# An mLSTM cell and an MLP in one kernel: where y of the twelve later units is transposed

## The chip, the cores and the metric

The kernel runs on one core of a Trainium2 chip. The metric is the device time of one execution in microseconds (us). Engines are named as in the profile: PE is TensorE (PEld its weight loads), DVE is VectorE, ACT is ScalarE, POOL is GpSimd, SP is SyncE, which here only issues DMAs.

## What is computed

An mLSTM cell over 4 batches, 8 heads, 768 steps and a head dimension of 40, followed by an MLP over 3072 tokens (320 features, 2048 hidden):

```python
def _attn_ref(q, k, v, i_gate, f_gate, o_gate):
    ...
    for t in range(S):
        ...
        m_new = np.maximum(f_gate[:, :, t] + m, i_gate[:, :, t])
        f_stab = np.exp(f_gate[:, :, t] + m - m_new)
        i_stab = np.exp(i_gate[:, :, t] - m_new)
        m = m_new
        C = f_stab[:, :, None, None] * C + i_stab[:, :, None, None] * np.einsum('bhd,bhe->bhde', vt, kt)
        n = f_stab[:, :, None] * n + i_stab[:, :, None] * kt
        h_tilde = np.einsum('bhde,bhe->bhd', C, qt)
        nq = np.einsum('bhd,bhd->bh', n, qt)[:, :, None]
        denom = np.maximum(np.abs(nq), 1.0)
        o = 1.0 / (1.0 + np.exp(-o_gate[:, :, t]))
        y[:, :, t] = o * h_tilde / denom
    return y
...
    x = np.ascontiguousarray(attn_out.transpose(0, 2, 1, 3)).reshape(B * S, H * D)
    h = x @ w_in
    g = h - np.tanh(h)
    return (g @ w_out).astype(np.float32)
```

Everything is float32.

## The kernel before

**Units and groups.** The tokens are cut into 24 units of 128 (a chunk of one batch; unit n is chunk n // 4 of batch n % 4). The cell of one unit makes `y`, 128 tokens by 320 features, tokens in the partitions. The MLP works on groups of two units (12 groups of 256 tokens) and needs x with features in the partitions. Six tiles `xT` (L324), each 128 partitions by 3 blocks by 256 tokens, hold it, one to a group in turn (group g uses `xT[g % 6]`). The three blocks start at the features in `FROM` (L276): 0, 128 and 192. The last two overlap; the second is read at its lower 64 rows and the third at its upper 64, as a half-height product each.

**The cell of a unit.** `scores` (L620) makes q times k by heads in PSUM (`ps` in the profile), a mask brings it to SBUF as `P`; `inter` and `intra` (L654, L663) add the state's part and the chunk's own part in `ph`; `gate` (L668) divides and multiplies by the output gate on VectorE and leaves `y` in one of two tiles `ys`; `update` (L694) computes the new state in `pc`, which `keep_state` (L702) adds and scales on VectorE. Then x: `turn` (L711) transposes one 128-column block of `y` on TensorE into PSUM tile `px`, and the third call ends with `keep_x` (L719), a ScalarE copy of 128 by 384 into the unit's half of `xT`.

**PSUM in the later part.** `ph`, `pc` and `px` come from `small` (L312), which takes turns over the banks named in `banks`. From L1374 on, one of the two serves the MLP's sums and the list has one name, so these three tiles follow each other in one bank.

**The MLP of an item.** An item is two pairs of 128-column blocks of the hidden layer, for one group. `up` (L897) makes `ph_up` from `xT` and `w_in`: 8 full-height products and 4 half-height ones, 24 passes in the profile. `shrink` squares on ScalarE (`z`, `q`), then VectorE makes `gt` in two steps, first out of `ph_up` and `z`, then out of `q`; `sums_of_g` (L770) makes the sums `s`, and `down_seven` (L785) multiplies into `pS` in 14 products, 28 passes, one item later.

**Order of the work.** Units 0 to 11 are laid out by a planner with costs (class Plan, L157); the change does not touch it. From item START on, the loop at L1376 merges two lists by hand: the dense products of an item, and the steps of a slot. A slot (s, o) with o = s - 1 covers two items; it finishes unit o and loads and prepares the next ones. `cell_slot` (L723) lists a slot's steps with a cost in us: inter and intra, gate, five pauses, three updates and four pauses (units 12 to 19), three turns, pauses, `prepare(s)`. `spread_over` (L1361) sets them at equal distances over the two items, and `merge` (L1011) places each at its share of the item's dense cost. `Clock` (L135) adds up the costs and releases the steps that `shrink` put off. Each engine runs its instructions in the order in which they are issued by these lists (L96 to L133), each engine by itself: an engine waits only where it needs another's result or a free buffer.

**SP's queue.** `load_unit` (L342) issues a unit's ten loads (seven where k is not needed) on SP at the beginning of a slot, for unit s + 1: kz and qz in two halves each, v, k, o, and q by heads in three parts (`q2`). The tiles have three buffers (o four), and SP issues a load as soon as its buffer is free. SP does nothing else in this stretch; the outputs go out on ACT's queue.

**A second path.** L1502 to the end recomputes all in a general way if a bound on the arguments fails; it is not run with these inputs, and it keeps using `turn`.

Of the kernel before, what the change touches and what calls it, by code (L numbers as in the profile page):

```python
# [49 lines left out]
FP = mybir.dt.float32  # L50
# [10 lines left out]
L = 128  # L61
# [18 lines left out]
def kernel(  # L80
# [33 lines left out]
    V, A, SP, G = Pinned(nc.vector), Pinned(nc.scalar), Pinned(nc.sync), Pinned(nc.gpsimd)  # L114
# [161 lines left out]
    FROM = (0, 128, DM - 128)  # L276
    NK = 2
    HALF = 64
    assert FROM[1] + HALF == FROM[2]
    NU = B * NT  # L280
    GT = 2
# [15 lines left out]
    NX = FIRST + 2  # L297
# [3 lines left out]
    dram = ctx.enter_context(tc.tile_pool(name="dram", bufs=1, space=bass.MemoryType.DRAM))  # L301
    att = ctx.enter_context(tc.tile_pool(name="att", bufs=2))
# [9 lines left out]
    def small(shape, name):  # L312
        banks.append(banks.pop(0))
        return ps_b.tile(shape, FP, name=name, tag=banks[-1])
# [9 lines left out]
    xT = [const.tile([128, NK + 1, TG], FP, name=f"xT{i}") for i in range(NX)]  # L324
# [17 lines left out]
    def load_unit(n, names=("kz", "qz", "v", "k", "o", "q2"), queue=SP, behind=()):  # L342
        c, b = divmod(n, B)
        t = ld.setdefault(n, {})
        for name in names:
            if name in ("kz", "qz"):
                t[name] = load.tile([128, HH, L], FP, name=name, tag=name, bufs=3)
                for i in range(2):
                    src = kT if name == "kz" else qT
                    dma = queue.dma_start(out=t[name][i * HALF:i * HALF + D], in_=src[b, c, :, i * HH:(i + 1) * HH])  # L350
                    if behind:
                        tc.add_manual_dep(dma.ins, behind[-1].ins.name, SYNC, reason="order of transfers")
            elif name == "k":
                if n + B < NU:
                    t["k"] = load.tile([L, WIDE, D], FP, name="k", tag="k", bufs=3)
                    queue.dma_start(out=t["k"].rearrange("p h d -> p (h d)"),
                                    in_=bass.AP(k.tensor, k[b, c].offset, [[H * D, L], [1, WIDE * D]]))
            elif name != "q2":
                src, bufs = {"v": (v, 3), "o": (o_gate, 4)}[name]
                t[name] = load.tile([L, H, D], FP, name=name, tag=name, bufs=bufs)  # L360
                queue.dma_start(out=t[name], in_=src[b, c])
            elif c:
                t["q2"] = load.tile([TOP, len(TRIOS), L], FP, name="q2", tag="q2", bufs=3)
                for i in range(TRIO):
                    queue.dma_start(out=t["q2"][i * D:(i + 1) * D, 0:len(range(i, H, TRIO))], in_=qT[b, c, :, slice(i, H, TRIO)])
# [204 lines left out]
    part = [parts_of[n // GT][:, n % GT] for n in range(FIRST * GT)]  # L570
# [3 lines left out]
    un = {}  # L574
# [12 lines left out]
    def begin(n):  # L587
        if n in ld:
            arrive(n)

        un[n]["P"] = att.tile([L, 2, HH, L], FP, name="P", tag="P", bufs=4)
# [5 lines left out]
    def prepare(n, whole=True, by_heads=False):  # L597

        t = un[n]
        if "vs" in t:  # L600
            return
        t["vs"] = scaled(n, 0, "vs", 4, by_heads)
        if whole:
            t["column"]()
            open_gate(n)
# [48 lines left out]
    def inter(n, j):  # L654
        t = un[n]
        if "ph" not in t:
            t["ph"] = small([L, H, D1], "ph")
        if t["c"]:
            rows = slice(0, len(TRIOS[j]) * D)
            T.matmul(trio(t["ph"], j), t["qs"][rows, j, :], trio(state[t["b"]][t["c"] % 2][rows], j), start=(j == 0), stop=False,  # L660
                     skip_group_check=True)

    def intra(n, h):  # L663
        t = un[n]
        T.matmul(t["ph"][:, h, :], t["P"][:, h // HH, h % HH, :], t["vs"][:, h, :], start=(t["c"] == 0 and h == 0), stop=True,
                 skip_group_check=True)

    def gate(n, in_parts=False):  # L668

        t = un[n]  # L670
        ph, sg = t["ph"], t["o"]
        den = att.tile([L, H], FP, name="den", tag="den")


        def over():
            V.scalar_tensor_tensor(out=den, in0=ph[:, :, D], scalar=-1.0, in1=inv[:, t["c"], t["hs"]], op0=OP.mult, op1=OP.max)
            V.tensor_tensor(out=den, in0=den, in1=ph[:, :, D], op=OP.max)
            V.reciprocal(out=den, in_=den)

        def shares():  # L680
            for h in range(H):
                A.mul(out=sg[:, h], in_=sg[:, h], mul=den[:, h:h + 1])

        def product():
            y = t["y"] = ys[n % 2]
            V.tensor_tensor(out=y.rearrange("p (h d) -> p h d", d=D), in0=ph[:, :, 0:D], in1=sg, op=OP.mult)

        if in_parts:
            return over, shares, product
        over()  # L690
        V.tensor_tensor(out=sg, in0=sg, in1=den.unsqueeze(2).to_broadcast([L, H, D]), op=OP.mult)
        product()

    def update(n, j, at_once=True):  # L694
        t = un[n]
        if j == 0:
            t["pc"] = small([TOP, H, D1], "pc")
        T.matmul(trio(t["pc"], j), t["k"][:, TRIO * j:TRIO * (j + 1)].rearrange("p h d -> p (h d)"), trio(t.get("vs_end", t["vs"]), j), start=True, stop=True)
        if j == len(TRIOS) - 1 and at_once:
            keep_state(n)  # L700
# [10 lines left out]
    def turn(n, j, at_once=True):  # L711
        t = un[n]
        if j == 0:
            t["px"] = small([128, NK + 1, L], "px")
        T.transpose(t["px"][:, j, :], t["y"][:, FROM[j]:FROM[j] + 128], ident)
        if j == NK and at_once:
            keep_x(n)

    def keep_x(n):  # L719
        g, tt = divmod(n, GT)  # L720
        A.copy(out=xT[g % NX][:, :, tt * L:(tt + 1) * L], in_=un[n]["px"])

    def cell_slot(s, o):  # L723


        steps, pause = [], [(0.0, lambda: None)]
        if o is not None:
            prepare(o)
        if s is not None:
            if s + 1 < NU and s + 1 not in ld:  # L730
                load_unit(s + 1)
            begin(s)
        if o is None:
            return [(0.0, lambda: prepare(s))]
        for d, heads in enumerate(TRIOS):
            steps.append((0.22 if o >= B else 0.0, lambda d=d: inter(o, d)))
            steps += [(0.22, lambda h=h: intra(o, h)) for h in heads]
        steps.append((0.0, lambda: gate(o)))
        steps += 5 * pause
        if o + B < NU:  # L740
            steps += [(0.2, lambda j=j: update(o, j)) for j in range(len(TRIOS))] + 4 * pause
        steps += [(0.11, lambda j=j: turn(o, j)) for j in range(NK + 1)] + 2 * pause
        if s is not None:
            steps.append((0.0, lambda: prepare(s)))
        return steps + 2 * pause
# [151 lines left out]
    def up(some, shrink):  # L897

        n = len(some)
        ph = [ps_h.tile([128, 2, TG], FP, name="ph_up", tag=f"ph{i}") for i in range(2)]  # L900

        def product(i, x, j):
            g, p = some[x]
            f = 2 * p + i
            at = ((0, 2, 1), (0, 1, 2))[i][j]
            if j < NK:
                col = (i, 3 - i)[j]
                lhs, rhs = w_in[:, p, col * 128:(col + 1) * 128], xT[g % NX][:, at, :]
            else:
                rows = slice(i * HALF, (i + 1) * HALF)  # L910
                lhs, rhs = w_in[rows, p, 2 * NK * 128:], xT[g % NX][rows, at, :]
            T.matmul(ph[i][:, x, :], lhs, rhs, start=(x == 0 and j == 0), stop=(j == NK), skip_group_check=True)

        full = [(0.43, lambda i=i, x=x, j=j: product(i, x, j)) for i in range(2) for x in range(n) for j in range(NK)]
        rest = [lambda i=i, x=x: product(i, x, NK) for x in range(n) for i in range(2)]
        return full, (rest, [lambda: shrink(some, ph)])
# [185 lines left out]
    of_tokens, of_states, exponentials, rows = {}, {}, [], []  # L1102
# [131 lines left out]
    for p in range(SPLIT, NP):  # L1234
        steps = []
# [266 lines left out]
    with tc.If(loaded[0] > 0):  # L1502
# [17 lines left out]
        for g in range(NG):  # L1520
# [19 lines left out]
            for p0 in range(0, NP, 2):  # L1540
                gts = []
                full, half = up(((g, p0), (g, p0 + 1)), lambda _, phs: gts.extend(shrink_any(ph) for ph in phs))
# [8 lines left out]
            for tt in range(GT):  # L1551
                o = mlp.tile([128, 5, HM], FP, name="ob", tag="ob")[:, 0:2].rearrange("p two n -> p (two n)")
# [43 lines left out]
```

## Time and profile before

| | us |
|---|---|
| median of 3 runs | 537.22 |
| lowest, highest | 537.08, 545.9 |
| profiled execution | 536.48 |
| its span, first to last instruction | 534.7 |
| units 12 to 23 (slots), in the span | some 231 to 474 |
| one slot (two items) with an update | 21.26 |
| mean granted TensorE clock | 0.996 |

The page gives busy times of each engine, the span in 40 slices, the DMA queues, the chain of work that ended last, and the costliest groups of instructions. A group's row has the engine, operation, output and input tiles, shape, count, then busy time in us, mean ns of one, and the idle time of the engine ahead of it with what ended it. In the timeline the first number is the start, the second the length, both in us; in brackets stands the idle time before it. A float32 product appears as two passes, a transpose as one: three transposes of 24 units are 72 matmuls. L106 and L129 are helpers that record every instruction, so the tiles' names tell the groups apart.

These groups of 231 to 474 us say what the engines do beside the cell's chain:

```profile
L106 DVE SCALAR_TENSOR_TENSOR gt<-q,gt 128x512 f32<-128x512 f32 x48 | 31.4, 683 | 0.0
L106 DVE SCALAR_TENSOR_TENSOR gt<-ph_up,z 128x512 f32<-128x512 f32 x48 | 30.8, 683 | 31.2 <-ACT z L106 31.2
L106 DVE TENSOR_TENSOR P<-ps,upto 128x512 f32<-128x512 f32 x21 | 13.6, 686 | 57.0 <-PE ps L129 57.0
L106 ACT COPY xT<-px 128x384 f32<-128x384 f32 x12 | 5.7, 472 | 0.0
```

VectorE spends most of its time on gt, and waits for ScalarE's z and TensorE's ps.

### The profile page before, as it was taken

How to read it: one execution, taken by the hardware profiler on the slowest of the kernel's cores; microseconds unless marked ns; L12 is line 12 of the kernel's file. 1: busy time of each engine (PE TensorE's matmuls, PEld its weight loads, DVE VectorE, ACT ScalarE, POOL GpSimd, SP SyncE). 2: the span in 40 equal slices, each digit the busy share in tenths (PEclk: the TensorE clock that was granted, in tenths of full speed). 3: DMA queues.
4: the chain of work that ended last, by engine and by line, in shares of the span. 5: the costliest groups of instructions: out<-in, count | busy, mean ns of one | idle time of the engine just before them, and what ended most of it. 6: DMA issues, size and time to landing. Idle time of an engine off the chain costs nothing.

```text
span 534.7 us, 9279 instructions
## 1 busy us (share of the span) xinstructions
PE 527.0 (99%) x3541; PEld 461.4 (86%) x3541; DVE 355.0 (66%) x768; ACT 204.3 (38%) x521; POOL 36.0 (7%) x63
## 2 busy tenths in 40 slices
PE   8999999999999999999999999999999999999996
PEld 5778878888798889889998998999999989988885
DVE  4999889988757666855853854756646546555544
ACT  4475696655442424223213312332242233232312
POOL 4523233100000000000000000000000000000000
PEclk8999999999999999999999999999999999999999
DMA  7987656331210001011302202111110000000001
GB/s 230 277 247 221 186 158 192 116 112 38 75 40 26 25 16 48 25 43 35 101 2 74 89 14 89 61 46 42 38 50 13 2 26 0 1 26 0 26 1 29
DMA packets 28137, 37.97 MB, mean 71 GB/s; under 512 B 3576, under 2 KB 21816, under 8 KB 28088
## 3 DMA queue, kind: packets, MB, share of 16 engines
q1 hardware_dynamic: 21856, 22.57, 14.6%
q0 software_dynamic: 3040, 10.82, 6.5%
q10 hardware_dynamic: 3192, 3.93, 2.2%
q8 instruction: 30, 0.49, 0.4%
q14 instruction: 19, 0.16, 0.1%
HBM read 33.37 MB, written 3.93 MB: 70 GB/s over the span
## 4 chain that ended last, share of the span: by engine, by line
PE 96%; DVE 1%; ACT 1%; POOL 1%; DMA 0%; issue 0%; SPq 0%; DVEq 0%
PE ph_up L129 41%; PE pS L129 30%; PE ph L129 9%; PE po L129 7%; PE ps L129 4%; PE pc L129 2%; PE px L133 2%; PE awake L129 1%; DMA w_out<-in_i_gate 0%; POOL w L106 0%; ACT vs L106 0%; DVE w_in L106 0%; ACT L106 0%; PE gate L129 0%; POOL P L106 0%; DVE den L106 0%
## 5 line engine op out<-in xcount | busy, mean ns | idle before, releaser
L129 PE MATMUL ph_up<-xT,w_in 128*128 128x256 f32 (+1 forms) x1152 | 245.2, 391 | 0.0
L129 PEld LDWEIGHTS ph_up<-xT,w_in 128*128 128x128 f32 (+1 forms) x1152 | 169.0, 189 | 28.7 <-issue 12.2
L106 ACT ACTIVATE z<-ph_up 128x512 f32<-128x512 f32 (+1 forms) x98 | 56.7, 583 | 255.9 <-PE ph_up L129 138.6
L106 DVE SCALAR_TENSOR_TENSOR gt<-ph_up,z 128x512 f32<-128x512 f32 (+1 forms) x98 | 63.4, 675 | 79.4 <-ACT z L106 79.1
L129 PE MATMUL pS<-wT,s 128*128 128x160 f32 x480 | 73.1, 300 | 0.0
L129 PEld LDWEIGHTS pS<-wT,s 128*128 128x128 f32 x480 | 67.5, 190 | 0.0
L106 DVE TENSOR_TENSOR P<-ps,upto 128x512 f32<-128x512 f32 x36 | 23.3, 686 | 66.5 <-PE ps L129 66.5
L106 ACT ACTIVATE q<-z,tiny 128x512 f32<-128x512 f32 (+1 forms) x98 | 66.2, 711 | 1.0
L106 DVE SCALAR_TENSOR_TENSOR gt<-q,gt 128x512 f32<-128x512 f32 (+1 forms) x98 | 63.4, 681 | 0.0
L129 PEld LDWEIGHTS ph<-vs,P 128*128 128x128 f32 x384 | 56.9, 191 | 5.7 <-POOL P L106 0.9
L129 PE MATMUL pS<-w_out,gt 128*128 128x160 f32 x320 | 56.8, 310 | 0.0
L129 PE MATMUL ph<-vs,P 128*128 128x41 f32 x384 | 55.4, 261 | 0.4 <-POOL P L106 0.4
L129 PEld LDWEIGHTS pS<-w_out,gt 128*128 128x128 f32 x320 | 46.1, 192 | 4.8 <-issue 3.6
L129 PE MATMUL po<-w_out,gt 128*128 128x320 f32 x128 | 38.2, 441 | 0.0
L129 PEld LDWEIGHTS po<-w_out,gt 128*128 128x128 f32 x128 | 23.1, 190 | 8.5 <-issue 0.3
L106 DVE TENSOR_TENSOR s<-gt 128x256 f32<-128x256 f32 x80 | 30.2, 418 | 0.0
L129 PE MATMUL pS<-wT,gt 128*128 128x160 f32 x160 | 29.2, 301 | 0.0
L129 PE MATMUL pS<-w_out,s 128*128 128x160 f32 x160 | 28.3, 299 | 0.0
L129 PEld LDWEIGHTS ps<-qz,kz 40*128 40x128 f32 x384 | 25.8, 191 | 2.2 <-DVE vs L106 0.8
L129 PE MATMUL ps<-qz,kz 40*128 40x128 f32 x384 | 26.6, 277 | 0.0
L129 PEld LDWEIGHTS pS<-w_out,s 128*128 128x128 f32 x160 | 23.9, 190 | 0.0
L129 PEld LDWEIGHTS pS<-wT,gt 128*128 128x128 f32 x160 | 23.8, 190 | 0.0
(93 smaller groups left out, 476.2 us busy)
## 6 DMA issues: line engine op xcount, KB each, us to landing
w<-in_moe_w_out POOLq DMA_DIRECT2D x8, 640.0 KB, 6.2
w<-in_moe_w_in POOLq DMA_DIRECT2D x16, 256.0 KB, 4.5
kz<-in_kT SPq DMA_DIRECT2D x48, 80.0 KB
o<-in_o_gate SPq DMA_DIRECT2D x24, 160.0 KB
k<-in_k SPq DMA_DIRECT2D x20, 180.0 KB
qz<-in_qT SPq DMA_DIRECT2D x44, 80.0 KB
v<-in_v SPq DMA_DIRECT2D x22, 160.0 KB
out<-ob ACTq DMA_DIRECT2D x11, 320.0 KB
```

The source lines that it names most:

```text
L106: i = method(*args, **kwargs)
L129: return cls.keep(nc.tensor.matmul(*args, **kwargs))
L133: return cls.keep(nc.tensor.transpose(*args, **kwargs))
```

## The change

In `cell_slot` the three `turn` steps of cost 0.11 become one step of cost 0, `turn_by_store`. It turns y's blocks of 32 by 32 on VectorE into a tile `yt`: each block is transposed where it stands, so partition 32 a + i, block b, column j holds feature 32 b + i of token 32 a + j. Four DMAs on SP, one for each 32 partitions, write the blocks into a DRAM tile `y_rows` of 384 features by 128 tokens, in runs of 32 tokens (128 B); two more DMAs on SP read the rows into the two halves of the partitions of `xT`. `yt` has two buffers, `y_rows` four. The planner's units and the second path keep `turn` and `keep_x`.

```diff
+    BLOCK = 32
+    NB = (NK + 1) * 128 // BLOCK
+
+    def turn_by_store(n):
...
+        y, g, tt = un[n]["y"], *divmod(n, GT)
+        yt = att.tile([L, NB, BLOCK], FP, name="yt", tag="yt")
+        flat = yt.rearrange("p b j -> p (b j)")
+        V.transpose(flat[:, 0:NK * 128], y[:, 0:NK * 128])
+        V.transpose(flat[:, NK * 128:], y[:, FROM[NK]:])
+        rows = dram.tile([(NK + 1) * 128, L], FP, name="y_rows", tag=f"y_rows{n % 4}")
+        for a in range(L // BLOCK):
+            part = slice(a * BLOCK, (a + 1) * BLOCK)
+            SP.dma_start(out=rows[:, part].rearrange("(b i) j -> i b j", i=BLOCK), in_=yt[part])
+        for i in range(2):
+            half = slice(i * HALF, (i + 1) * HALF)
+            SP.dma_start(out=xT[g % NX][half, :, tt * L:(tt + 1) * L], in_=rows.rearrange("(c p) t -> p c t", p=128)[half])
+
     def cell_slot(s, o):
...
-        steps += [(0.11, lambda j=j: turn(o, j)) for j in range(NK + 1)] + 2 * pause
+        steps += [(0.0, lambda: turn_by_store(o))] + 2 * pause
         if s is not None:
             steps.append((0.0, lambda: prepare(s)))
         return steps + 2 * pause
```

## Prediction

> **What bounds the kernel now.** I read the page from the top: busy times, the clock row, the chain of waits.
>
> ```profile
> ## 1 busy us (share of the span) xinstructions
> PE 527.0 (99%) x3541; PEld 461.4 (86%) x3541; DVE 355.0 (66%) x768; ACT 204.3 (38%) x521; POOL 36.0 (7%) x63
> ...
> PEclk8999999999999999999999999999999999999999
> ...
> PE 96%; DVE 1%; ACT 1%; POOL 1%; DMA 0%; issue 0%; SPq 0%; DVEq 0%
> PE ph_up L129 41%; PE pS L129 30%; PE ph L129 9%; PE po L129 7%; PE ps L129 4%; PE pc L129 2%; PE px L133 2%; PE awake L129 1%; DMA w_out<-in_i_gate 0%; POOL w L106 0%; ACT vs L106 0%; DVE w_in L106 0%; ACT L106 0%; PE gate L129 0%; POOL P L106 0%; DVE den L106 0%
> ```
>
> The chain that ended last is 96% TensorE at full clock. So a TensorE instruction taken away shortens the run by the time between starts that it took, and work on another engine costs nothing until TensorE waits for it. The list of waits for PE between 231 and 474 us, where the twelve later units run, is empty: there is no wait to remove, only work. The groups, with shapes kept apart, give the work that the change touches, for all 24 units:
>
> ```profile
> L133 PE MATMUL px<-ident,ys 128*128 128x128 f32 x72 | 16.4, 285 | 0.2 <-DVE ys L106 0.2
> L106 ACT COPY xT<-px 128x384 f32<-128x384 f32 x24 | 11.2, 476 | 13.5 <-PE px L133 13.5
> ```
>
> Half of each belongs to units 12 to 23. The 285 ns is a latency in a pipeline, not what the end would gain. What one set of three costs is read by comparing items (24 ph_up and 28 pS passes each) in TensorE's timeline; the first number is the start:
>
> ```profile
> 465.77 3.62 PE L129 MATMUL ph_up<-xT,w_in 128*128 128x256 f32 x16
> 469.22 0.27 PE L133 MATMUL px<-ident,ys 128*128 128x128 f32 x1
> ...
> 470.49 0.33 PE L133 MATMUL px<-ident,ys 128*128 128x128 f32 x1
> 470.66 0.71 PE L129 MATMUL pS<-w_out,gt 128*128 128x160 f32 x4
> 471.20 0.27 PE L133 MATMUL px<-ident,ys 128*128 128x128 f32 x1
> 471.31 0.71 PE L129 MATMUL pS<-w_out,gt 128*128 128x160 f32 x4
> ...
> 474.57 4.68 PE L129 MATMUL ph_up<-xT,w_in 128*128 128x256 f32 x24
> ...
> 483.09 4.68 PE L129 MATMUL ph_up<-xT,w_in 128*128 128x256 f32 x24
> ```
>
> The item with unit 23's three transposes lasts 474.57 - 465.77 = 8.80 us, the next, without any, 483.09 - 474.57 = 8.52. Three transposes cost **0.28 us**, not 3 x 0.285.
>
> **What the Trainium skill says.** "TensorE: Matmul & The Clock Gate", Part 4, puts a TensorE transpose inside a kernel at about 275 ns; the trace's median is 273. "VectorE: DVE Perf Modes", The three transpose paths, gives VectorE 311 ns for 128x128 in bf16 and says that it turns 32x32 blocks only, which is why the blocks must be put in their places by a transfer; no such instruction is in this trace. "DMA: Bandwidth & Descriptors", Specifications, says that under 512 B the engines read, modify and write; Anatomy of one DMA puts a fixed 2.0 us on each transfer, mostly the receipt of the write. The stores here have runs of 128 B; the trace has no such store to agree or not.
>
> **The change, part by part**, for each of 12 units.
>
> Removed from TensorE: three transposes, 0.28 us; 12 x 0.28 = 3.4 us. Bounds: the chain charges px 1.8% of 534.7 us over 24 units, 0.40 each, 4.8 in all, and part of that is a switch from the 64-row products that stays; 36 whole durations of 273 ns would be 9.8 us, which the overlap excludes. Below, nothing is gained if the gap stays. I take 3.4.
>
> Removed from ScalarE: a copy of 476 ns. ScalarE is 38% busy and not on the chain: 0.
>
> Removed from PSUM: px no longer takes the one rotating bank between pc and the next unit's ph. No wait there shows today: 0.
>
> Added on VectorE: turns of 128x256 and 128x128. Nearest rows: a product of 128x256 out of SBUF is 418 ns, a copy of 128x128 284; together **0.70 us**. The skill's 311 ns per block of 128 columns would give 0.93; at half that rate for four-byte data 1.87 (estimates). I take 0.7 and keep 0.6 to 1.9. They stand in VectorE's order after the state update and ahead of the next gt out of ph_up:
>
> ```profile
> 260.17 0.50 DVE L106 TENSOR_TENSOR state<-state,eT 120x328 f32<-120x328 f32 x1
> 261.99 1.29 DVE L106 SCALAR_TENSOR_TENSOR gt<-ph_up,z 128x512 f32<-128x512 f32 x2 [1.32 <-ACT z L106]
> ...
> 265.52 0.82 PE L129 MATMUL ph_up<-xT,w_in 128*128 128x256 f32 x3
> ```
>
> VectorE idles 1.32 us there, waiting for ScalarE's z, and 0.7 fits inside. Should it not, gt is late; the next product into that bank starts at 265.52, 2.24 us after gt ends at 263.28. So TensorE feels only what goes past 1.32 + 2.24 = 3.6 us. For units without an update the idle is 3.40 us (before gt at 410.29), for unit 23 1.73. Cost: 0. Its waits for y are on its own engine; behind it stand gt, s and vs, with their users an item away.
>
> Added on SP's queue: four stores and two loads. A head-sliced load takes 0.38 us to issue (three in 1.15), so 2.3 us in all. The first store waits for the turns; the first x load waits for all stores to land. Queued behind are the loads of unit o+3, which today go out as soon as buffers allow:
>
> ```profile
> 258.38 0.35 SPq L106 DMA_DIRECT2D k<-in_k  x1
> ...
> 260.76 0.71 SPq L106 DMA_DIRECT2D kz<-in_kT  x2
> ```
>
> k at 258.38 is unit 16's, released by unit 13's update; the kz behind it is already unit 17's. In the new order unit 16's kz waits for unit 13's round trip, unit 17's for unit 14's, a slot later than today. The round trip from the page's queue rows:
>
> ```profile
> q1 hardware_dynamic: 21856, 22.57, 14.6%
> q10 hardware_dynamic: 3192, 3.93, 2.2%
> ```
>
> 14.6% of 16 engines' 534.7 us over 21856 packets is 57 ns a packet; q10, which writes the output, has 59. Four stores are 4 x 384 = 1536 packets, 96 an engine: 5.5 us at 57 ns, 11 at double. The two x loads are 384 packets, 1.4 us. With 2 us fixed for the stores and again for the loads, x is in SBUF 1.6 + 2 + 5.5 + 0.8 + 2 + 1.4 = 13.3 us after the turns (18.8 at double).
>
> Who waits: group 6 begins with unit 13's x at 286.78 in TensorE's timeline; unit 13's turns end near 261.4: 25.4 us. Group 11 needs unit 23's at 491.61, the turns end near 470.4: 21.2 us. Unit 16's kz and qz, which follow the x loads, are needed at its scores, two slots of 21.26 us after unit 14's at 250.06, at 292.6: 31 us. All hold at 57 ns and, by 2 us at the least, at double. Cost: 0. The traffic, 0.39 MB more per slot of 21 us, is 19 GB/s beside the 53 GB/s that this stretch carries; the DMA row shows tenths of 0 to 6 there.
>
> Moved: three steps become one, so a slot has 30 steps where it had 32 (23 for 25, 22 for 24 at the end), spread over the same two items. The gate, step 11, goes from 0.34 to 0.37 of the slot, some 0.5 us later (0.8 to 0.9 in the shorter slots); the update shifts with it. The gate's y ended at 255.19 and its bank's next user, pc, started at 256.7: 1.5 us, which moves as a whole. The 0.33 us of planned cost that goes reorders nothing by itself. Cost 0, bounds -0.3 to +0.3 per unit (estimate from that margin), 3.6 either way.
>
> Sum: -3.4 + 0. Against its own execution: span 534.7 to 531.3, time 536.48 to 533.1. The median shown, 537.22, is 0.7 above that execution, so on the median's scale **533.8 us**, 0.6% down.
>
> **Rivals.**
>
> A, slower: the round trip through DRAM ends on the path. With 7.8 us of the sum above fixed or loads, group 6 waits once 96 packets take over 25.4 - 7.8 = 17.6 us, that is 183 ns each, 3.2 times the mean; group 11 from 140 ns. For: the 128 B writes, which no row prices. Against: 57 ns is for packets eight times as long. At 210 ns five groups wait 2.6 us and the last 6.8: +19.8 - 3.4, 553 us.
>
> B, slower: the four-byte turn is far slower on VectorE than its rows. It decides from 3.6 us a unit; at 5 us, 12 x 1.4 - 3.4 = +13, 551 us. Against: five times any comparable row.
>
> C, no change: the transposes fill gaps that stay, or the later gate makes TensorE wait some 0.3 us a unit: 537 to 538.
>
> D, more gained: the chain's charge for the two px sets between 240 and 264 us, 4.0% of 24 us, 0.48 a unit, is what goes: 5.8, 531.4. Past 2% down can't be reached by removing 9.8 us of durations.
>
> E, it does not do what it says: units 12 to 23 are all that cell_slot handles as o; if some kept the old way, the gain shrinks into C.
>
> **How the numbers follow.** Forecast, 532 to 536: 0.58. C and E, 536 to 541: 0.12. D, 530 to 532: 0.09. A 0.12 and B 0.05 past 546. A stray gain past 2%: 0.04, for what no view shows. The range 530 to 546 leaves out A, B and little else. 2%, some 10.7 us, is about what a measurement of this kernel can tell from no change: faster 0.04, within 0.79, slower 0.17.
>
> **What would show it.** 36 px matmuls in place of 72 and 12 fewer ScalarE copies; two VectorE turns a unit of 0.4 and 0.3 us, with the idle ahead of gt shorter by their sum; items of unit 23's kind at 8.52 us; no wait of PE on a DMA or on y's rows in 231 to 474. Wrong would be: a PE idle ahead of ph_up or ps named after a DMA (A) or after gt (B), or slots that stay 21.26 us long (C).

## The result, and the profile after

The changed kernel takes **533.87 us** (median of 23 runs) where the kernel before takes 536.77 in runs beside it (median of 23); the ratio is 0.9944, 95% interval 0.9928 to 0.9961. Two later sets of runs gave 0.9957 (0.9939 to 0.9975) and 0.9946 (0.9926 to 0.9967). Some executions of either kernel take about 10 us longer and count in the medians but not in the ratios; the first profile of the changed kernel is of one (span 540.7 us; TensorE's products took about twice as long in its first 30 us), so the lines below are of a second profile (span 529.9 us, run after_again).

The page, again busy times and chain:

```profile
PE 522.4 (99%) x3505; PEld 456.2 (86%) x3505; DVE 361.4 (68%) x792; ACT 200.0 (38%) x509; POOL 35.7 (7%) x63
...
PE ph_up L129 41%; PE pS L129 30%; PE ph L129 9%; PE po L129 7%; PE ps L129 4%; PE pc L129 2%; PE awake L129 1%; PE px L133 1%; DMA w_out<-in_i_gate 0%; ACT vs L106 0%; DVE w_in L106 0%; ACT L106 0%; PE gate L129 0%; DVE den L106 0%; DVE o L106 0%; DVE ys L106 0%
```

TensorE has 36 matmuls fewer, px fell from 2% of the chain to 1%, VectorE has 24 instructions more, and neither VectorE's turns (yt) nor a DMA of y_rows has come onto the chain. The groups, shapes apart:

```profile
L133 PE MATMUL px<-ident,ys 128*128 128x128 f32 x36 | 5.9, 278 | 0.2 <-DVE ys L106 0.2
L106 ACT COPY xT<-px 128x384 f32<-128x384 f32 x12 | 5.6, 482 | 11.7 <-PE px L133 11.7
L106 DVE STREAM_TRANSPOSE yt<-ys 128x256 f32<-128x256 f32 x12 | 5.3, 438 | 0.1
L106 DVE STREAM_TRANSPOSE yt<-ys 128x128 f32<-128x128 f32 x12 | 3.2, 269 | 0.0
```

36 px and 12 copies are left, all of the planner's units. A turn of 256 columns takes 438 ns, one of 128 takes 269. TensorE's timeline at unit 23, whose three transposes are gone:

```profile
461.01 4.68 PE L129 MATMUL ph_up<-xT,w_in 128*128 128x256 f32 x24
...
469.53 4.68 PE L129 MATMUL ph_up<-xT,w_in 128*128 128x256 f32 x24
...
478.04 4.68 PE L129 MATMUL ph_up<-xT,w_in 128*128 128x256 f32 x24
```

The item that was 8.80 us is now 8.52, like the one after it.

**A measure finer than the run's time.** The first 160 us, which the change leaves as they are, scatter by 4 us and more from run to run. In the chain of waits, the first whole item after the planner and the first whole item after the last slot can be found in each profile. Before:

```profile
162.44 4.52 PE ph_up L129 x24
...
474.74 4.52 PE ph_up L129 x24
```

and with the change:

```profile
160.20 4.52 PE ph_up L129 x24
...
469.69 4.52 PE ph_up L129 x24
```

The first number is the start. The stretch of all slots took 312.30 us before and takes 309.49, so 2.81 us went there. It is the same to 0.01 us in three profiles of the changed kernel, and it is what the experiments are compared by. Of the kernel before there is one profile.

| kernel | the slots' stretch, us | against before | ratio of times (95%) |
|---|---|---|---|
| before | 312.30 | | |
| the change | 309.49 | -2.81 | 0.9944 (0.9928 to 0.9961) |
| no_turn | 309.49 | -2.81 | 0.9936 (0.9914 to 0.9958) |
| one_step_turn | 313.30 | +1.00 | 1.0019 (1.0000 to 1.0038) |
| both_turns | 313.31 | +1.01 | 1.0021 (1.0004 to 1.0039) |
| turns_x4 | 309.48 | -2.82 | 0.9987 (0.9949 to 1.0025) |
| turns_x8 | 311.28 | -1.02 | 1.0004 (0.9975 to 1.0033) |
| stores_x4 | 309.49 | -2.81 | 0.9969 (0.9932 to 1.0005) |
| spaced | 308.84 | -3.46 | 0.9911 (0.9874 to 0.9947) |

In turns_x8 the first item after the slots is itself 0.26 us longer, so the start of the next is taken, less 8.52 us.

### The profile page after: what moved, and what is told of

Same layout as the page of the kernel before. It is cut to its first block, busy times and chain, and to the rows that moved or that the text cites. A ratio compares the mean times of both kernels' runs of the same rounds, so it can differ in the third digit from the quotient of the medians.

```text
span 540.7 us, 9346 instructions
## 1 busy us (share of the span) xinstructions
PE 534.0 (99%) x3505; PEld 464.4 (86%) x3505; DVE 361.5 (67%) x792; ACT 199.8 (37%) x509; POOL 35.8 (7%) x63
## 4 chain that ended last, share of the span: by engine, by line
PE 98%; ACT 1%; DVE 0%; issue 0%
PE ph_up L129 41%; PE pS L129 30%; PE ph L129 10%; PE po L129 7%; PE ps L129 5%; PE awake L129 3%; PE pc L129 2%; PE px L133 1%; ACT vs L106 0%; PE gate L129 0%; ACT L106 0%; PE gate L133 0%; DVE ob L106 0%; ACT part L106 0%; ACT o L106 0%; ACT ei L106 0%
## 5 line engine op out<-in xcount | busy, mean ns | idle before, releaser
L129 PEld LDWEIGHTS ph<-vs,P 128*128 128x128 f32 x384 | 59.8, 203 | 5.1 <-issue 1.2
L129 PE MATMUL ph<-vs,P 128*128 128x41 f32 x384 | 57.7, 272 | 0.0
L129 PEld LDWEIGHTS pS<-w_out,gt 128*128 128x128 f32 x320 | 45.0, 190 | 8.8 <-issue 5.6
L129 PEld LDWEIGHTS ps<-qz,kz 40*128 40x128 f32 x384 | 27.6, 205 | 2.2 <-DVE vs L106 0.8
L129 PE MATMUL ps<-qz,kz 40*128 40x128 f32 x384 | 28.7, 293 | 0.0
L129 PEld LDWEIGHTS pS<-w_out,s 128*128 128x128 f32 x160 | 23.9, 190 | 0.0
```

Source lines behind the costliest of these rows:

```text
L129: return cls.keep(nc.tensor.matmul(*args, **kwargs))
```

## Experiments

**The change again.**

> The changed kernel once more, for a profile beside the others of this call. Theory (the gain is TensorE's time for 36 transposes): 0.994 of the kernel before, 3.4 us less; 36 px matmuls; no wait of PE between the first and last slot; an item of unit 23's kind at 8.52 us in place of 8.80.

0.9957, 2.81 us in the stretch, 36 px, no wait of PE between 225 and 475 us. The item is 8.52. The gain is a little under the 3.4 us expected.

**What is removed, and the new spacing.** Three kernels take the change apart. one_step_turn keeps TensorE's transposes in the change's step:

```diff
-        steps += [(0.0, lambda: turn_by_store(o))] + 2 * pause
+        steps += [(0.0, lambda: [turn(o, j) for j in range(NK + 1)])] + 2 * pause
```

> The three turns stay on TensorE with ScalarE's copy, but as one step of cost 0 where the change has its step: so the slot has 30, 23 and 22 steps as in the change, and nothing of VectorE, SP or DRAM. Theory (TensorE's removed work is the gain): 1.000 of before, within 1 us. Rival (the new spacing of the slot's steps is the gain): 0.994, as the change.

both_turns does both:

```diff
-        steps += [(0.0, lambda: turn_by_store(o))] + 2 * pause
+        steps += [(0.0, lambda: [turn_by_store(o), *[turn(o, j, at_once=False) for j in range(NK + 1)]])] + 2 * pause
```

> The change, with the three TensorE transposes into px left in beside it (the copy to xT is left out, x comes through DRAM). Theory: the whole gain goes, 1.000 of before within 1 us. Rival (the gain is the freed copy, or px's bank wait): under 0.997.

no_turn leaves out both, and so the y of these units does not reach x:

```diff
-        steps += [(0.0, lambda: turn_by_store(o))] + 2 * pause
+        steps += 3 * pause
```

> No turn at all for units 12 to 23: the y of these units is not carried into x, groups 6 to 11 use what the xT tiles held. Theory (turns on VectorE and the trip through DRAM cost nothing): as the change within 0.5 us, 0.994. Rival (the change pays for its turns or transfers in part): faster than the change by 1 us or more, 0.992 or less.

The transposes left in beside the DRAM path take the whole gain away (1.0021), and the freed copy is worth nothing: one_step_turn, which has the copy, and both_turns, which lacks it, agree to 0.01 us in the stretch. The freed PSUM bank was not tested apart, since both of them use it for px. Neither they nor the kernel before have a wait of PE in their lists from 170 to 475 us, and the time of the transposes themselves, read below, leaves nothing for the bank. no_turn agrees with the change to 0.01 us, so VectorE's turns, six DMAs and the trip through DRAM cost **nothing that can be seen**. Between one_step_turn and the change lie 3.81 us, 0.32 for each unit's three transposes. The one point off is that one_step_turn is 1.00 us slower than before, at the limit of what was expected: three transposes in a row and 30 steps in place of 32 are a little worse than what the kernel before had. The run spaced below puts 0.65 us on the steps; the rest is not traced. TensorE's timeline of one_step_turn:

```profile
259.60 1.08 PE L129 MATMUL pS<-w_out,gt 128*128 128x160 f32 x6
260.51 0.49 PE L133 MATMUL px<-ident,ys 128*128 128x128 f32 x3
260.84 0.44 PE L129 MATMUL pS<-w_out,gt 128*128 128x160 f32 x2
```

The next pS starts 0.33 us after the first of three px, about the 0.32 lost for each unit.

**The cover of VectorE's turns.**

```diff
-        V.transpose(flat[:, 0:NK * 128], y[:, 0:NK * 128])
-        V.transpose(flat[:, NK * 128:], y[:, FROM[NK]:])
+        for _ in range(4):
+            V.transpose(flat[:, 0:NK * 128], y[:, 0:NK * 128])
+            V.transpose(flat[:, NK * 128:], y[:, FROM[NK]:])
```

> The change with each unit's two VectorE turns done four times over into the same tile (8 in place of 2, 2.8 us in place of 0.71). Theory (VectorE's idle before gt of 1.3 to 3.4 us, and 2.2 us from gt's end to the next product into its bank, cover up to 3.6 us): as the change, 0.995 of before. Rival (VectorE's added time is felt at once, only 0.7 us is too small to see): 2.1 us for each of 12 units more, +25 us, 1.04.

> As turns_x4, but eight times over: 5.7 us a unit. Theory: past the cover, 5.7 - 3.6 = 2.1 us for the odd units with an update, some 0.9 for the even ones, 0.2 for units 20 to 23: 13 us more than the change, 1.02 of before, with PE idle ahead of ph_up. Rival (other slack lies behind it): as the change. Rival (felt at once): +60 us.

Four times the turns change nothing in the stretch (309.48); the ratio of its few runs, 0.9987, carries a start that was late by 3.6 us in the profile. With eight times, the slots with an update take turns at 21.04 us (as with the change) and 21.36. The timeline of turns_x8, VectorE and TensorE, in one of the longer ones:

```profile
260.10 0.50 DVE L106 TENSOR_TENSOR state<-state,eT 120x328 f32<-120x328 f32 x1
260.51 4.27 DVE L106 STREAM_TRANSPOSE yt<-ys 128x256 f32<-128x256 f32 x16
...
264.71 1.25 DVE L106 SCALAR_TENSOR_TENSOR gt<-ph_up,z 128x512 f32<-128x512 f32 x2
...
265.41 1.13 PE L129 MATMUL ph_up<-xT,w_in 128*128 128x256 f32 x4
```

gt follows the turns without a gap, and now ends at 265.96, after ph_up has begun: the point where the cover ends is reached. The expected idle of PE ahead of ph_up is not in the list of waits. The delay shows inside the run: from the ph ahead of these four ph_up passes to the ph behind them lie 1.34 us (265.16 to 266.50), in the change 1.09. 16 turns take 4.27 us, not 5.7: back to back, a pair costs 0.53. With that number the expected rule holds roughly: 4.27 - 3.6 is some 0.7 us where 0.32 was felt, so the cover is nearer 3.9 us. The other slots with an update, expected at 0.9, feel nothing. Of the 1.8 us that the stretch grew, the four longer slots make 1.3, and units 21 and 23, which have no update, some 0.25 each. The expectation of +13 us failed mainly by its price for the turns.

**The slack of the trip through DRAM.**

```diff
-        for a in range(L // BLOCK):
+        for a in 4 * list(range(L // BLOCK)):
```

> The change with the four stores of a unit done four times over to the same rows, each after the one before has landed (16 DMAs and four receipts in place of one, some 3.4 us each by the change's trace: 14 us from the turns to the x loads). Theory (the trip has 25 us to group 6 and 21 to group 11, and SP needs 14 + 7 of the slot's 21 us): as the change, 0.995. Rival (the trip through DRAM is close to the path): 10 us for each group or more, 1.05 and up.

> As stores_x4, but six times over: 20 us and 7 more for the loads, 27 us of SP's queue for each unit against a slot of 21. Theory: the queue falls 6 us behind for each unit, uses up some 25 us of lead, and then TensorE waits for DMAs in every slot: 12 x 6 - 25 = some 45 us more, 1.08, PE idle named after DMAs. If it is as the change, the prediction's rival A was further off than worked out.

Four rounds of stores are free (309.49), six are not: 1.0424 (1.0371 to 1.0477). Where it waits, in the list of PE's waits of stores_x6 (total, times, longest):

```profile
PE ph_up L129 <- DMA xT<-y_rows: 9.3, 3, 3.5
PE ps L129 <- DMA qz<-in_qT: 2.5, 2, 1.3
PE ph_up L129 <- DVE s L106: 0.3, 1, 0.3
```

Both of the places named for rival A come up: a group's first product, and scores whose loads stand behind the round trip on SP's queue. The end comes 25 us later than with the change, 45 were expected; the stores of successive units begin 23.9 us apart (237.33 to 380.75 over six units), where 27 were worked out. So the queue fell behind by 3 us for each slot of 21, not 6. By the same rule that makes 12 x 3 - 25 = 11 us, and the waits in the list come to 12.1. TensorE also ran at half its clock for some 20 us in all after the waits (last section), by an estimate from the clock in the trace another 9.6 us. The last 3 us are not traced.

**The old spacing with the new turn.** Two more pauses give each slot its 32, 25 and 24 steps back.

```diff
-        steps += [(0.0, lambda: turn_by_store(o))] + 2 * pause
+        steps += pause + [(0.0, lambda: turn_by_store(o))] + 3 * pause
```

> The change with two more pauses in a slot, one ahead of the new step and one behind: 32, 25 and 24 steps at the places of the kernel before, the new step where the second turn stood. Theory (the removal is worth 0.28 us or more in every slot, and the new spacing gives back some 0.08 us in each of the 8 slots with an update): those slots at 20.95 us against 21.04 with the change and 21.25 before; the part from the first undivided item at 162 us to the end at 369.0 against 369.7 and 372.3. Rival (the smaller gain in slots with an update is the removal's own): 21.04 and 369.7, as the change.

The stretch is 308.84, 0.65 less than with the change, and 3.46 less than before; the slots with an update last 20.97 us against 21.04 and 21.25. The chain of waits shows what the spacing does to one such slot. The change:

```profile
246.05 1.57 PE ph_up L129 x10
...
248.51 0.83 PE ph L129 x6
249.34 0.58 PE pS L129 x4
249.92 0.15 PE ph L129 x2
250.07 0.62 PE pS L129 x4
250.69 0.15 PE ph L129 x2
250.84 2.79 PE pS L129 x20
```

and spaced:

```profile
246.18 0.51 PE ph_up L129 x2
246.69 0.15 PE ph L129 x2
246.84 1.06 PE ph_up L129 x8
...
248.79 0.79 PE ph L129 x6
249.59 0.62 PE pS L129 x4
250.20 0.15 PE ph L129 x2
250.35 3.33 PE pS L129 x24
```

The columns are start, length, work. Two ph passes that in the change stand among the 28 pS passes stand in spaced among the ten ph_up passes ahead (at 246.69). The pS passes take 3.99 us in three pieces and 3.95 in two, and the six ph ahead of them 0.83 against 0.79: 0.08 us in all, close to the 0.07 between the slots. The ten ph_up passes take 1.57 us in one piece and 0.51 + 1.06 in two: there the same break costs nothing. Nothing waits. So what a break costs depends on the place; why these two places differ is not shown.

**Going further.** spaced_early also sends units 9, 10 and 11 of the planner's part through DRAM, with a VectorE step for the turns and two SP steps in the plan:

```diff
+    STORED = (9, 10, 11)
...
+        if n in STORED:
+            u["turn"] = plan.add("V", 0.75, lambda: turn_blocks(n), [u["gate"]], rank)
+            u["rows"] = plan.add("S", 1.9, lambda: store_rows(n), [u["turn"]], rank, kb=196, small=True)
+            u["x"] = plan.add("S", 0.8, lambda: load_rows(n), [u["rows"]], rank, kb=196, small=True)
+        else:
...
```

> As spaced, and units 9, 10 and 11 of the planner's part go through DRAM too, in the plan as a VectorE step and two SP steps. Theory: three more sets of TensorE transposes at some 0.3 us, 0.9 us less than spaced, 0.992 of the kernel before. Rival (the planner moves other work and loses or wins more than that): anything from 0.988 to 1.000, not told from the part after 162 us, which stays as in spaced.

0.9925 (0.9904 to 0.9946): no gain over spaced can be told. Its stretch is that of spaced; whether the first 160 us gained the expected 0.9 us is lost in their scatter and stays open.

Last, the change and spaced beside each other on one chip.

> The changed kernel on the same chip as spaced_beside. Theory: the part from the first undivided item to the end at 369.4 to 369.7 us; 0.994 to 0.996 of the kernel before.

> spaced once more, beside the change on one chip. Theory: 0.6 us less up to the end of the slots (308.84 from the first undivided item, against 309.49), 0.7 to 1.1 us less in all, 0.992 to 0.994 of the kernel before. Rival (its lead was the chip's or the start's): no lead, the same ratio as change_beside.

0.9946 (0.9926 to 0.9967) and 0.9930 (0.9911 to 0.9948), medians 532.37 and 531.65 us; the stretch again 309.49 and 308.84. The run times put spaced ahead in both sets, but their intervals overlap; the stretch, the same to 0.01 us in each kernel's profiles, shows the 0.65 us. By that little spaced is faster than the change.

## Why the prediction held

**The bound.** TensorE stayed 99% busy without a wait in the slots. Right, and both_turns shows that it was TensorE's instructions that paid: no gap stayed in their place, as rival C had it.

**The removal, 3.4 us at 0.28 a set.** With the spacing held as before (spaced), it is 3.46 us in the stretch, 0.29 a set. The chain's charge of 0.40 and rival D (5.8 us) were too high; reading the difference between two items was the better price.

**ScalarE's copy and PSUM's bank, 0.** Right for the copy: one_step_turn and both_turns agree. For the bank nothing speaks against it: no wait of PE before, and the transposes' own time explains the loss when they are put back.

**VectorE's turns, 0.70 us and covered.** 0.71 by the durations of the rows, 0.63 as a pair. In the place that the prediction showed:

```profile
257.57 0.50 DVE L106 TENSOR_TENSOR state<-state,eT 120x328 f32<-120x328 f32 x1
257.99 0.63 DVE L106 STREAM_TRANSPOSE yt<-ys 128x256 f32<-128x256 f32 x2
...
259.61 1.29 DVE L106 SCALAR_TENSOR_TENSOR gt<-ph_up,z 128x512 f32<-128x512 f32 x2 [0.99 <-ACT z L106]
```

The turns fill part of the idle time, and 0.99 us of it is left. That is 0.33 less than before only because the new spacing alone makes this idle longer, 1.54 us in no_turn; from there the turns take 0.55. With the old spacing (spaced) they leave 0.77 of 1.32 us, 0.55 again. turns_x8 found the end of the cover near 3.9 us for 3.6 forecast. The trace is faster than the figure of "VectorE: DVE Perf Modes", The three transpose paths, 311 ns for 128x128 in bf16: it has 269 ns in float32.

**The trip through DRAM, 13.3 us and covered.** Right in kind and too long. SP's timeline:

```profile
258.64 2.85 SPq L106 DMA_DIRECT2D y_rows<-yt  x4
263.00 1.25 SPq L106 DMA_DIRECT2D xT<-y_rows  x2
264.29 0.90 SPq L106 DMA_DIRECT2D kz<-in_kT  x2
```

From the first store's issue to the first x load's there are 4.4 us here, where one store took 1.5 us to issue, and 3.3 to 3.6 for the other eleven units; 1.6 + 2 + 5.5 = 9.1 were forecast. The main term at fault is the packet: 57 ns was the mean of packets eight times as long. SP's queue on the page of the change, and of stores_x6, which adds stores alone:

```profile
q1 hardware_dynamic: 46048, 27.29, 18.9%
q1 hardware_dynamic: 142048, 39.11, 32.2%
```

18.9% of 16 engines' 529.9 us is 1602 us; before it was 14.6% of 534.7, 1249 us for 21856 packets. The 24192 packets that came, stores and x loads, cost 353 us, 15 ns each. In stores_x6 32.2% of 16 engines' 555.3 us is 2861 us: 96000 packets more than with the change, all for stores, for 1259 us, 13 ns each. So a unit's 96 packets an engine cost some 1.3 us in place of 5.5. "DMA: Bandwidth & Descriptors", Specifications, led to doubling the price of a packet under 512 B. The packet was cheaper, not dearer; but by the byte the stores did cost nearly double, 0.11 ns (1259 us for 11.82 MB) against 0.055 before (1249 us for 22.57 MB), so the trace does not contradict the page. From the end of the last store's issue to the x load there are 1.5 us (261.49 to 263.00) where 2 + 5.5 were added, so the fixed part behind the issue is at most 1.5. The page's section Anatomy of one DMA, from which the 2 us came, is about transfers that GpSimd issues; these go out from SP. When x lands is not in the profile of the change; in stores_x6 a product that waits for x starts 3.6 us after the first x load's issue (326.49 to 330.06), where 4.2 were forecast.

That rival A decides at some point, and where its waits would stand, stores_x6 showed; where the point lies was not measured in packet time.

**The moved steps, 0 within 0.3 a unit.** Inside the bound, but not 0: 0.65 us in all were given back, some 0.07 in each slot with an update, by a break that fell among the pS passes as in the slot shown. The prediction looked for a wait there and found none, rightly; it did not price where the breaks in TensorE's runs fall. This accounts for the 0.6 us between the change's 2.81 and the forecast's 3.4.

**The time.** 533.8 forecast, 533.87 measured. That the two agree so closely is luck: by the medians the gain was 2.90 us where 3.4 were forecast, and the median of the kernel before was 0.45 us lower in 23 runs than in the 3 that the forecast started from. The two misses cancel.

## What to carry to other kernels

Where one engine is busy throughout, price what is taken from it by the difference between two repeats of the same work with and without it, not by the durations of its instructions: 0.28 us here for three of 0.285 each. Then work on other engines, and even a trip through DRAM, is free as long as it ends before anything waits for it, here within 25 us for a trip whose stores take 3.3 to 4.4. And when steps are taken out of a hand-spread list, the rest moves: keep the places with pauses, and compare stretches of the trace that are the same in every run when the whole time scatters more than the effect.

## What the runs showed of the hardware that was not expected

A store in runs of 128 B cost some 13 ns a packet of a DMA engine's time, against a mean of 57 on the same queue before, with packets of 1033 B on average: a quarter by the packet, nearly double by the byte.

And a wait can cost TensorE more than its length. In stores_x6:

```profile
326.63 0.38 PE L129 MATMUL ph<-state,q 120*128 120x123 f32 x2
330.06 2.04 PE L129 MATMUL ph_up<-xT,w_in 128*128 128x256 f32 x4 [3.04 <-DMA xT<-y_rows]
```

After 3.04 us of idling, four ph_up passes took 2.04 us where they take 1.03 without the wait. The granted clock, the share of TensorE's full clock that the trace records, is 0.50 from 330 to 335 us, 1.00 before the wait and 1.00 again from 336. Of the five waits for DMAs in this trace four, of 1.19, 1.29, 3.04 and 3.54 us, are followed by such a stretch of 3 to 7 us at 0.50, and one, of 2.72 us, is not. So the length of the wait alone does not decide it, and what does is not shown.
